# The opening of an attention and MLP mix, reordered: x rounded first, q's second tile moved into the main loop

## The chip, the cores and the metric

The kernel runs on one core of a Trainium2 chip. The core has five engines with an instruction queue each: TensorE (PE, with its weight loads listed apart as PEld), VectorE (DVE), ScalarE (ACT), GpSimd (POOL) and SyncE (SP, which here only issues DMAs). Each queue runs in order, and queues wait for each other through semaphores. The metric is the device time of one execution in microseconds, lower is better. Before the change it is 1294.38 us, the median of three runs.

## The reference

The output mixes two branches of the same input x (2048 positions, 512 features) with a gate per position:

```
g = sigmoid((x * gate_w).sum(-1, keepdims=True))
# branch a: 32 heads of 16 share one k and one v
q = heads(x @ wq);  k = x @ wk;  v = x @ wv
p = softmax(q @ k.T * 16**-0.5)          # 2048 x 2048 for each head
a = (p @ v, heads joined) @ wo
# branch b: 1792 hidden features
r = max(x @ w1 + b1, 0)
b = (r * r) @ w2 + b2
out = g * a + (1 - g) * b
```

All arrays are float32. wq and wk are scaled up by about 36, so scores are large and the softmax needs a shift.

## The kernel before, in words

Products are made in split form: each operand is rounded to the matmul's float format (the r tiles) and the rest of it is kept in a second tile (the l tiles); a product is three matmuls, r by r, l by r and r by l. `xsplit` does this for x (L271): ACT writes xr, and DVE or POOL subtracts to get xl. `wq_split` (L375) does the same for a quarter of wq.

The opening, L386 to L424, is written out in order, and that order is the order on each queue. x comes in four chunks of 512 positions. `kv` (L277) makes k, v and the gate's product for a chunk by 12 matmuls, and three ACT copies of the result: its square, `kvs` and `kb`. `k_parts` (L288) writes the chunk of `k_aug`, the weights of the scores. `kv_rest` (L296) makes the norms of k and turns v over by narrow matmuls, and DVE copies v into `v_ext` and the gate's sums into `z`. The maximum over all norms of k gives the softmax's shift, `km2`, which `k_shift` (L292) writes into rows of k_aug: no score can be made before all four chunks' norms are known.

q is made in tiles of 128 features (8 heads) by one chunk (L312, `qproj`): 12 matmuls, a rounding, a rest, a square, and stores to DRAM (`qs`). `qnorm` (L339) makes q's norms with one matmul and an approximate root and stores them too. `q_load` (L355) reads a group of four heads back in six DMAs, as the scores need it (`qa`). Sixteen tiles of q serve 32 groups. Two tiles, q0 and q1, are made in the opening ("early", with whole matmuls); the other fourteen are made among the scores, with matmuls in pairs on the two halves of the array (`mm2`).

The main loop (L683 to L704) goes over 1024 units, 32 for each group. A unit is `scores` (L496: two matmuls and one exp on ACT) and later its share of `context` (L510). It runs in phases: a phase takes one small chore from a list (`chores`), then two or three units' scores with a piece of the other work between them (`work`, L605: q's tiles, then the MLP, then the output product), then the context of the units of the phase before. A generator says after each piece whether the next phase takes three units (FULL) or two (LIGHT). TensorE runs what it is given in that order. PSUM holds two scores tiles (`sp`), one context accumulator (`ap`) and three others (`mp`).

Before the opening's first real matmul stand 12 matmuls on zeros (`WARM`, L389), which write the accumulator's bank.

Of the kernel before, what the change touches and what calls it, by code (L numbers as in the profile page):

```python
# [135 lines left out]
def mix_kernel(ctx: ExitStack, tc: tile.TileContext, xT, wkv, wq, wo, w12, b1, b2, cst, out):  # L136
# [29 lines left out]
    def pairs(ar, al, br, bl):  # L166
        return [(ar, br), (ar, bl), (al, br)]
# [51 lines left out]
    with fast, tc.tile_pool(name="at", bufs=1) as at, \  # L219
# [7 lines left out]
        xf = {}  # L227

        def x_load(c):
            for a in range(2):  # L230
                if a == 0:
                    both = at.tile([128, KT, CH], F32, name="xf", tag="e", bufs=3)
# [12 lines left out]
        x_load(3)  # L245
        wq_load(slice(128, D))
# [12 lines left out]
        nc.vector.memset(ones, 0.0)  # L259
        nc.vector.memset(ones[:16], 1.0)  # L260
        nc.vector.memset(v_ext, 1.0)

        def run(gen):
            while True:
# [3 lines left out]
                    return e.value  # L268


        def xsplit(c):  # L271
            for a, eng in enumerate((nc.vector, nc.vector if c < 2 else nc.gpsimd)):
                ks = slice(2 * a, 2 * a + 2)
                nc.scalar.activation(xr[c][:, ks], xf[c, a], AF.Copy)
                eng.tensor_tensor(xl[c][:, ks], xf[c, a], xr[c][:, ks].bitcast(F32), OP.subtract)

        def kv(c):  # L277
            ps = mp.tile([128, CH], F32, name="mm")
            mm(ps, [t for k in range(KT) for t in pairs(wkr[:, k], wkl[:, k], xr[c][:, k], xl[c][:, k])])
            kvs = at.tile([128, CH], F32, name="kvs", tag="h", bufs=2)  # L280
            kb = at.tile([128, CH], F32R, name="kb", tag="of", bufs=8)
            sq = at.tile([96, CH], BF, name="sqk", tag="sq", bufs=2)
            nc.scalar.activation(sq, ps[:96], AF.Square)
            nc.scalar.activation(kvs, ps, AF.Copy)
            nc.scalar.activation(kb, kvs, AF.Copy)
            return kvs, kb, sq

        def k_parts(c, kvs, kb, sq):  # L288
            nc.vector.scalar_tensor_tensor(k_aug[:, c * CH:(c + 1) * CH], kb.bitcast(F32), cs[:, C_A:C_A + 1], kvs,
                                           op0=OP.mult, op1=OP.add)  # L290

        def k_shift(c):  # L292
            for p in (RS, 64 + RS):
                nc.vector.tensor_copy(k_aug[p:p + 1, c * CH:(c + 1) * CH], km2[p:p + 1, 0:1].to_broadcast([1, CH]))

        def kv_rest(c, kvs, kb, sq):  # L296
            pn = sp.tile([128, 2, CH], F32, name="s")
            nc.tensor.matmul(pn[:, 0], ones, sq, start=True, stop=True)
            for j in range(4):
                nc.tensor.matmul(pn[:, 1, j * 17:(j + 1) * 17], kvs[:, j * 128:(j + 1) * 128],  # L300
                                 cs[:, C_SEL:C_SEL + 17], start=True, stop=True)
            nc.vector.tensor_reduce(kmx[:, c:c + 1], pn[:, 0], AX.X, OP.max)
            vz = pn[:, 1, :68].rearrange("p (j d) -> p j d", j=4)
            nc.vector.tensor_copy(v_ext[:, 4 * c:4 * c + 4, 0:32:2], vz[:, :, :DH])
            nc.vector.tensor_copy(z[:, 4 * c:4 * c + 4], vz[:, :, DH])

        def root(dst, src, tmp):

            nc.vector.tensor_scalar(tmp.bitcast(I32), src.bitcast(I32), 0.5, ROOT, op0=OP.mult, op1=OP.add)
            nc.vector.tensor_copy(dst, tmp)  # L310

        def qproj(c, t, early=False):  # L312
            cols = slice(t * 128, (t + 1) * 128)
            terms = [u for k in range(KT) for u in
                     pairs(wqr[:, k, cols], wql[:, k, cols], xr[c][:, k], xl[c][:, k])]
            qr = at.tile([128, CH], F32R, name="qr", tag="of", bufs=8)
            ql = at.tile([128, CH], F32R, name="ql", tag="of", bufs=8)
            sq = at.tile([128, CH], BF, name="sq", bufs=2)
            if early:
                q = mp.tile([128, CH], F32, name="mm")  # L320
                mm(q, terms)
                nc.scalar.activation(qr, q, AF.Copy)
            else:
                ps = [mp.tile([128, CH], F32, name="mm") for _ in range(2)]
                yield from mm2(*ps, terms, 6)
                q = at.tile([128, CH], F32, name="qf", tag="of", bufs=8)
                nc.vector.tensor_copy(q, ps[0])
# [3 lines left out]
            nc.vector.tensor_tensor(sq, qr.bitcast(F32), qr.bitcast(F32), OP.mult)  # L331
            it = c * NG + 2 * t
            for src, row, eng in ((qr, 0, nc.sync), (ql, DH + 1, nc.sync if early else nc.gpsimd)):
                o = qs[it, 0, row]
                eng.dma_start(bass.AP(tensor=o.tensor, offset=o.offset,
                                      ap=[[KS * 2 * CH, 4], [CH, 2 * DH], [1, CH]]), src.bitcast(F32))
            return it, sq

        def qnorm(it, sq):  # L339
            p8 = mp.tile([128, CH], F32, name="mm")  # L340
            nc.tensor.matmul(p8[:8], blk, sq, start=True, stop=True)  # L341
            nrm = at.tile([8, CH], F32R, name="nrm", bufs=2)
            tmp = at.tile([8, CH], F32, name="tmp", tag="n")
            nc.vector.tensor_copy(tmp, p8[:8])
# [30 lines left out]
        def wq_split(t, eng):  # L375
            cols = slice(t * 128, (t + 1) * 128)
            nc.scalar.activation(wqr[:, :, cols], wqf[:, :, cols], AF.Copy)
            eng.tensor_tensor(wql[:, :, cols], wqf[:, :, cols], wqr[:, :, cols].bitcast(F32), OP.subtract)

        def gate():  # L380
            for o, s in ((g, -1.0), (omg, 1.0)):
# [3 lines left out]

        wu = at.tile([128, CH], BF, name="wu", tag="sq", bufs=2)  # L386
        nc.vector.memset(wu, 0.0)
        pw = ap.tile([128, CH], F32, name="acc")
        for _ in range(WARM):  # L389
            nc.tensor.matmul(pw, wu[:, :128], wu, start=True, stop=True)  # L390
        split(wkr, wkl, wkvf)
        xsplit(0)
        nc.vector.tensor_copy(blk, cs[:, C_BLK:C_BLK + 8])
        xsplit(1)
        k0 = kv(0)
        k_parts(0, *k0)
        wq_split(0, nc.vector)
        xsplit(2)
        k1 = kv(1)
        kv_rest(0, *k0)  # L400
        xsplit(3)
        k_parts(1, *k1)
        q0 = run(qproj(0, 0, early=True))
        k2 = kv(2)
        kv_rest(1, *k1)
        k3 = kv(3)
        qnorm(*q0)
        kv_rest(2, *k2)
        kv_rest(3, *k3)
        nc.vector.tensor_reduce(km, kmx, AX.X, OP.max)  # L410
        root(km2, km, km2)
        nc.vector.tensor_scalar(km2, km2, -1.0, None, op0=OP.mult)
        for c in range(2):
            k_shift(c)
        for t in range(1, 4):
            wq_split(t, nc.gpsimd)
        q_load(0)
        k_parts(2, *k2)
        k_shift(2)
        q1 = run(qproj(0, 1, early=True))  # L420
        k_parts(3, *k3)
        k_shift(3)
        gate()
        w_load(0)  # L424


        chores = []

        def by_now(what, f):
            while f not in what:  # L430
# [223 lines left out]

        side, lazy = [], work()

        def phase(us):
# [30 lines left out]
        while us:  # L688
# [4 lines left out]
            kind = phase(nxt)  # L693
            if k == 0:
                acc = ap.tile([128, CH], F32, name="acc")
            while narrow:
# [72 lines left out]
```

## Time and profile before

| what | us |
|---|---|
| median of three runs | 1294.38 (1293.84 to 1295.3) |
| the profiled execution, its own time | 1294.1 |
| its span, first to last instruction | 1292.2 |
| TensorE busy | 1263.2 (98%) |
| ScalarE busy | 1030.8 (80%) |
| VectorE busy | 625.8 (48%) |
| GpSimd busy | 58.9 (5%) |
| both halves of the first scores, start | 38.09 |

Times in the profile are counted from the span's start; an instruction's line (L503) is that of the kernel. In the chain of waits each step is what released the next. In groups of instructions the columns are line, engine, operation, output and inputs with shapes, count, busy us and mean ns, and then the engine's idle time ahead of them and what ended it. The timeline gives the start, the length, and the same names, with the idle time in brackets.

### The profile page before, as it was taken

How to read it: one execution, taken by the hardware profiler on the slowest of the kernel's cores; microseconds unless marked ns; L12 is line 12 of the kernel's file. 1: busy time of each engine (PE TensorE's matmuls, PEld its weight loads, DVE VectorE, ACT ScalarE, POOL GpSimd, SP SyncE). 2: the span in 40 equal slices, each digit the busy share in tenths (PEclk: the TensorE clock that was granted, in tenths of full speed). 3: DMA queues.
4: the chain of work that ended last, by engine and by line, in shares of the span. 5: the costliest groups of instructions: out<-in, count | busy, mean ns of one | idle time of the engine just before them, and what ended most of it. 6: DMA issues, size and time to landing. Idle time of an engine off the chain costs nothing.

```text
span 1292.2 us, 25244 instructions
## 1 busy us (share of the span) xinstructions
PE 1263.2 (98%) x10722; PEld 642.5 (50%) x10722; DVE 625.8 (48%) x1117; ACT 1030.8 (80%) x1084; POOL 58.9 (5%) x66
## 2 busy tenths in 40 slices
PE   8899999999999999999999999999999999999996
PEld 5455555555555555555555555555554433322232
DVE  6567855546555464464645547457580304020212
ACT  5677787777877777777777777877779999999984
POOL 2010150200000000000000000000000000000000
PEclk9899999999999999999999999999999999999998
DMA  6233311000101000110011000121001120110100
GB/s 207 79 92 90 93 39 38 30 14 34 38 22 47 15 27 26 39 46 15 16 38 38 30 14 33 38 88 62 18 13 39 46 78 31 53 38 22 54 1 35
DMA packets 29661, 57.36 MB, mean 44 GB/s; under 512 B 8936, under 2 KB 10600, under 8 KB 29544
## 3 DMA queue, kind: packets, MB, share of 16 engines
q1 hardware_dynamic: 23288, 44.40, 10.6%
q0 software_dynamic: 5968, 10.77, 2.6%
q8 instruction: 86, 1.41, 0.4%
q10 hardware_dynamic: 288, 0.52, 0.1%
q14 instruction: 31, 0.25, 0.1%
HBM read 31.02 MB, written 16.78 MB: 37 GB/s over the span
## 4 chain that ended last, share of the span: by engine, by line
PE 91%; ACT 5%; DVE 1%; DMA 1%; issue 1%; SPq 0%; ACTq 0%; DVEq 0%
PE acc L518 35%; PE mm L179 30%; PE s L503 23%; ACT e L507 5%; PE mm L171 1%; DMA xf<-in_xT 1%; DMA qa<-qs 1%; PE mm L341 0%; PE s L171 0%; DMA qs<-nrm 0%; DVE res L468 0%; PE mm L568 0%; PE s L300 0%; ACT accs L545 0%; DVE al L541 0%
## 5 line engine op out<-in xcount | busy, mean ns | idle before, releaser
L507 ACT ACTIVATE e<-s 128x1024 f32<-128x1024 f32 x1024 | 998.5, 1024 | 228.4 <-PE s L503 178.9
L518 PE MATMUL acc<-e,v_ext 128*32 128x512 f32 (+1 forms) x5128 | 524.8, 514 | 0.7 <-ACT e L507 0.7
L503 PE MATMUL s<-qa,k_aug 49*128 49x512 f32 x2048 | 452.5, 439 | 13.0 <-ACT e L507 9.5
L503 PEld LDWEIGHTS s<-qa,k_aug 49*128 49x128 f32 x2048 | 193.7, 184 | 329.7 <-ACT e L507 217.2
L518 PEld LDWEIGHTS acc<-e,v_ext 128*32 128x32 f32 x5128 | 129.2, 108 | 223.4 <-issue 194.3
L468 DVE SCALAR_TENSOR_TENSOR res<-mm,omg,res 128x512 f32<-128x512 f32 x224 | 168.2, 751 | 132.7 <-PE mm L179 119.6
L449 DVE TENSOR_SCALAR h<-mm,b1t 128x512 f32<-128x512 f32 x56 | 42.0, 751 | 208.1 <-PE mm L179 208.1
L179 PE MATMUL mm<-w2r,hr 64*128 64x512 f32 x448 | 91.5, 397 | 0.1
L179 PE MATMUL mm<-w2l,hr 64*128 64x512 f32 x448 | 90.3, 392 | 0.0
L179 PE MATMUL mm<-w2r,hl 64*128 64x512 f32 x448 | 89.7, 390 | 0.0
L179 PE MATMUL mm<-xr,w1l 64*128 64x512 f32 x448 | 88.7, 393 | 0.0
L179 PE MATMUL mm<-xr,w1r 64*128 64x512 f32 x448 | 88.2, 391 | 0.0
L179 PE MATMUL mm<-xl,w1r 64*128 64x512 f32 x448 | 88.2, 390 | 0.0
L209 DVE SCALAR_TENSOR_TENSOR ot<-mm,g,res 128x512 f32<-128x512 f32 x12 | 9.0, 752 | 120.2 <-PE mm L179 120.2
L532 DVE RECIPROCAL n<-n 128x128 f32<-128x128 f32 x60 | 57.2, 953 | 2.1
L529 DVE TENSOR_SCALAR n<-lc 128x128 f32<-128x128 f32 x60 | 13.3, 221 | 75.8 <-DMA lc<-accs 75.3
L179 PEld LDWEIGHTS mm<-w2r,hl 64*128 64x128 f32 x448 | 43.4, 184 | 10.4
L179 PEld LDWEIGHTS mm<-w2l,hr 64*128 64x128 f32 x448 | 43.8, 187 | 8.9
L561 POOL DMA_DIRECT2D oTs<-oc x15 | 8.3, 551 | 871.2 <-DVE oc L533 861.1
L179 PEld LDWEIGHTS mm<-xl,w1r 64*128 64x128 f32 x448 | 42.5, 186 | 9.7
L179 PEld LDWEIGHTS mm<-w2r,hr 64*128 64x128 f32 x448 | 44.2, 187 | 5.9 <-DVE res L468 0.9
L179 PEld LDWEIGHTS mm<-xr,w1l 64*128 64x128 f32 x448 | 41.9, 184 | 9.5
(127 smaller groups left out, 776.6 us busy)
## 6 DMA issues: line engine op xcount, KB each, us to landing
qa<-qs SPq DMA_DIRECT2D x128, 64.0 KB
wf<-in_w SPq DMA_DIRECT2D x14, 512.0 KB
qa<-qs SPq DMA_DIRECT2D x64, 68.0 KB
xf<-in_xT SPq DMA_DIRECT2D x8, 512.0 KB
qs<-qr SPq DMA_DIRECT2D x16, 256.0 KB
oc<-accs SPq DMA_DIRECT2D x30, 128.0 KB
lc<-accs SPq DMA_DIRECT2D x30, 128.0 KB
oTs<-oc POOLq DMA_DIRECT2D x15, 256.0 KB, 2.3
```

Of the source, the lines that this page charges most:

```text
L171: nc.tensor.matmul(ps, a, b, start=first and i == 0, stop=last and i == len(terms) - 1)
L179: nc.tensor.matmul(ps, a[rows], b[rows], start=i == 0, stop=i == len(terms) - 1)
L209: nc.vector.scalar_tensor_tensor(ot, ps[0], g[:, s:s + 1], res[c][:, j], op0=OP.mult, op1=OP.add)
L449: nc.vector.tensor_scalar(h, ps[0], b1t[:, f:f + 1], None, op0=OP.add)
L468: nc.vector.scalar_tensor_tensor(res[c][:, j], p, omg[:, s:s + 1], res[c][:, j], op0=OP.mult, op1=OP.add)
L503: nc.tensor.matmul(s[:, r].rearrange("p (a n) -> p a n", a=2), k_aug[rows, kt * 128:(kt + 1) * 128], qa[it][rows, :, cols], start=True, st ...
L507: nc.scalar.activation(es[u // 2][:, :, cols], s.rearrange("p r (a n) -> p (r a) n", a=2), AF.Exp, scale=SCALE)
L518: nc.tensor.matmul(acc[h * 32:(h + 1) * 32, cols], v_ext[:, i % NK], es[i][:, h % 2 * 2 + h // 2, cols], start=(i % NK == 0), stop=(i % NK ...
L529: nc.vector.tensor_scalar(n[:, cols], l[:, cols], L_MIN, L_MAX, op0=OP.max, op1=OP.min)
L532: nc.vector.reciprocal(n[:, cols], n[:, cols])
L561: nc.gpsimd.dma_start(oTs[it - 1:it + 1].rearrange("u d n -> (u d) n"), o)
```

## The change

The opening is rewritten; the main loop's body is nearly the same.

- x: the fourth chunk gets a buffer of its own (tag "r3"), so that all loads are issued ahead; wq's first quarter is loaded right after x's first chunk. All subtractions for xl and wql are on DVE; three memsets go to POOL.
- Order: k's chunk 0, then q0 at once, then the other chunks; a chunk's matmuls come in two halves, and the roundings of x are put between them. The load of q's first group, `q_load(0)`, is issued before k's third and fourth chunks are done.
- q0's square is made by ACT; the root is taken straight from PSUM, without a copy first.
- v's narrow matmuls write the accumulator's bank (`pv`), and the copies into v_ext and z stand together at the end of the opening.
- The matmuls on zeros are 24 of 240 columns, in the same bank beside `pv` (`pw`), and 24 more stand at the end of the opening, ahead of the first scores.
- Only chunk 0 of k_aug is written in the opening. Chunks 1 to 3, the third and fourth quarter of wq and the gate become chores of the first five phases.
- q1 is no longer made early: `work` begins with it, as the first of fifteen tiles.
- The loop begins with two units instead of three, and the first phase puts its first scores after a piece of q1's matmuls.

```diff
+            both = keep.tile(sh, F32, name="xf", tag="r3") if c == NC - 1 else \
+                at.tile(sh, F32, name="xf", tag="e", bufs=3)
...
         x_load(0)
+        wq_load(slice(0, 128))
         nc.sync.dma_start(cs, cst)
         x_load(1)
-        wq_load(slice(0, 128))
...
+        def kv(c, a):
+            if a == 0:
+                pks[c] = mp.tile([128, CH], F32, name="mm")
+            mm(pks[c], [t for k in (2 * a, 2 * a + 1)
+                        for t in sorted(pairs(wkr[:, k], wkl[:, k], xr[c][:, k], xl[c][:, k]),
+                                        key=lambda t: t[1] is xl[c])], first=a == 0, last=a == 1)
+        def kv_out(c):
+            sq = at.tile([96, CH], BF, name="sqk", tag="sq", bufs=2)
+            nc.scalar.activation(sq, pks[c][:96], AF.Square)
+            kvs[c] = at.tile([128, CH], F32, name="kvs", tag="of", bufs=8)
+            nc.scalar.activation(kvs[c], pks[c], AF.Copy)
+            return sq
...
+        def v_part(c):
+            for j in range(4):
+                nc.tensor.matmul(pv[:, c, j * 17:(j + 1) * 17], kvs[c][:, j * 128:(j + 1) * 128],
+                                 cs[:, C_SEL:C_SEL + 17], start=True, stop=True)
+        def v_out(c):
+            vz = pv[:, c].rearrange("p (j d) -> p j d", j=4)
+            nc.vector.tensor_copy(v_ext[:, 4 * c:4 * c + 4, 0:32:2], vz[:, :, :DH])
+            nc.vector.tensor_copy(z[:, 4 * c:4 * c + 4], vz[:, :, DH])
...
             if early:
                 nc.scalar.activation(qr, q, AF.Copy)
+                nc.scalar.activation(sq, qr.bitcast(F32), AF.Square)
...
-            nc.vector.tensor_copy(tmp, p8[:8])
-            root(nrm, tmp, tmp)
+            root(tmp, p8[:8])
+            nc.vector.tensor_copy(nrm, tmp)
...
+        ps = ap.tile([128, CH], F32, name="acc")
+        pv, pw = ps[:, :272].rearrange("p (c n) -> p c n", c=NC), ps[:, 272:]
+        def warm(n):
+            for _ in range(n):
+                nc.tensor.matmul(pw, wu[:, :128], wu[:, 272:], start=True, stop=True)
+        warm(2 * WARM)
         split(wkr, wkl, wkvf)
+        xsplit(0, 0)
+        xsplit(0, 1)
+        kv(0, 0)
+        kv(0, 1)
+        wq_split(0)
+        xsplit(1, 0)
+        xsplit(1, 1)
+        sq0 = kv_out(0)
         nc.vector.tensor_copy(blk, cs[:, C_BLK:C_BLK + 8])
+        xsplit(2, 0)
         q0 = run(qproj(0, 0, early=True))
+        kv(1, 0)
+        kv(1, 1)
+        k_norm(0, sq0)
+        xsplit(2, 1)
         qnorm(*q0)
+        xsplit(3, 0)
+        sq1 = kv_out(1)
+        kv(2, 0)
+        k_norm(1, sq1)
+        xsplit(3, 1)
+        q_load(0)
+        kv(2, 1)
+        sq2 = kv_out(2)
+        kv(3, 0)
+        k_norm(2, sq2)
+        kv(3, 1)
+        k_parts(0)
+        wq_split(1)
+        sq3 = kv_out(3)
+        for c in range(3):
+            v_part(c)
+        k_norm(3, sq3)
         nc.vector.tensor_reduce(km, kmx, AX.X, OP.max)
...
+        k_shift(0)
+        v_part(3)
+        for c in range(NC):
+            v_out(c)
+        warm(2 * WARM)
+        w_load(0)
+        def k_rest(c):
+            k_parts(c)
+            k_shift(c)
+        chores = [lambda: k_rest(1), lambda: k_rest(2), lambda: (k_rest(3), wq_split(2)), lambda: wq_split(3), gate]
...
-            prev = q1
-            for i in range(2, 16):
+            prev = None
+            for i in range(1, 16):
                 q = yield from qproj(*divmod(i, 4))
-                narrow.append(prev)
+                if prev:
+                    narrow.append(prev)
...
-            if us:
+            if us and not start:
                 scores(us.pop(0))
...
-        kind = FULL
+        kind = LIGHT
```

More of the change, by code (lines that the diff above doesn't have):

```diff
@@ L258, in mix_kernel @@
         z = at.tile([128, NS], F32, name="z")
-        nc.vector.memset(ones, 0.0)
-        nc.vector.memset(ones[:16], 1.0)
-        nc.vector.memset(v_ext, 1.0)
+        nc.gpsimd.memset(ones, 0.0)
+        nc.gpsimd.memset(ones[:16], 1.0)
+        nc.gpsimd.memset(v_ext, 1.0)
         def run(gen):
@@ L268, in run @@
                     return e.value
[L271 to L280, printed above, removed]
-            kb = at.tile([128, CH], F32R, name="kb", tag="of", bufs=8)
[L282 to L286, printed above, removed]
@@ L288, in k_parts, with xsplit @@
-        def k_parts(c, kvs, kb, sq):
-            nc.vector.scalar_tensor_tensor(k_aug[:, c * CH:(c + 1) * CH], kb.bitcast(F32), cs[:, C_A:C_A + 1], kvs,
-                                           op0=OP.mult, op1=OP.add)
+        def xsplit(c, a):
+            ks = slice(2 * a, 2 * a + 2)
+            nc.scalar.activation(xr[c][:, ks], xf[c, a], AF.Copy)
+            nc.vector.tensor_tensor(xl[c][:, ks], xf[c, a], xr[c][:, ks].bitcast(F32), OP.subtract)
+        kvs, pks, pn = {}, {}, []
+        def kv(c, a):
[4 more added lines that the diff above has]
+                                        key=lambda t: t[1] is xl[c])], first=a == 0, last=a == 1)
@@ new lines, in kv_out, with k_parts @@
+        def kv_out(c):
[4 more added lines that the diff above has]
+            return sq
+        def k_parts(c):
+            kb = at.tile([128, CH], F32R, name="kb", tag="of", bufs=8)
+            nc.scalar.activation(kb, kvs[c], AF.Copy)
+            nc.vector.scalar_tensor_tensor(k_aug[:, c * CH:(c + 1) * CH], kb.bitcast(F32), cs[:, C_A:C_A + 1],
+                                           kvs[c], op0=OP.mult, op1=OP.add)
@@ L294, in k_shift, with k_norm, root @@
                 nc.vector.tensor_copy(k_aug[p:p + 1, c * CH:(c + 1) * CH], km2[p:p + 1, 0:1].to_broadcast([1, CH]))
-        def kv_rest(c, kvs, kb, sq):
-            pn = sp.tile([128, 2, CH], F32, name="s")
-            nc.tensor.matmul(pn[:, 0], ones, sq, start=True, stop=True)
+        def k_norm(c, sq):
+            if c < 2:
+                pn.append(sp.tile([128, 2, CH], F32, name="s"))
+            p = pn[c % 2][:, c // 2]
+            nc.tensor.matmul(p, ones, sq, start=True, stop=True)
+            nc.vector.tensor_reduce(kmx[:, c:c + 1], p, AX.X, OP.max)
+        def v_part(c):
             for j in range(4):
-                nc.tensor.matmul(pn[:, 1, j * 17:(j + 1) * 17], kvs[:, j * 128:(j + 1) * 128],
+                nc.tensor.matmul(pv[:, c, j * 17:(j + 1) * 17], kvs[c][:, j * 128:(j + 1) * 128],
                                  cs[:, C_SEL:C_SEL + 17], start=True, stop=True)
-            nc.vector.tensor_reduce(kmx[:, c:c + 1], pn[:, 0], AX.X, OP.max)
-            vz = pn[:, 1, :68].rearrange("p (j d) -> p j d", j=4)
+        def v_out(c):
+            vz = pv[:, c].rearrange("p (j d) -> p j d", j=4)
             nc.vector.tensor_copy(v_ext[:, 4 * c:4 * c + 4, 0:32:2], vz[:, :, :DH])
             nc.vector.tensor_copy(z[:, 4 * c:4 * c + 4], vz[:, :, DH])
-        def root(dst, src, tmp):
-            nc.vector.tensor_scalar(tmp.bitcast(I32), src.bitcast(I32), 0.5, ROOT, op0=OP.mult, op1=OP.add)
-            nc.vector.tensor_copy(dst, tmp)
+        def root(dst, src):
+            nc.vector.tensor_scalar(dst.bitcast(I32), src.bitcast(I32), 0.5, ROOT, op0=OP.mult, op1=OP.add)
         def qproj(c, t, early=False):
@@ L373, in w_split, with wq_split @@
             split(*dst[f], wf[f][:, half * 512:half * 512 + 512])
-        def wq_split(t, eng):
+        def wq_split(t):
             cols = slice(t * 128, (t + 1) * 128)
             nc.scalar.activation(wqr[:, :, cols], wqf[:, :, cols], AF.Copy)
-            eng.tensor_tensor(wql[:, :, cols], wqf[:, :, cols], wqr[:, :, cols].bitcast(F32), OP.subtract)
+            nc.vector.tensor_tensor(wql[:, :, cols], wqf[:, :, cols], wqr[:, :, cols].bitcast(F32), OP.subtract)
         def gate():
@@ L387, in mix_kernel @@
         nc.vector.memset(wu, 0.0)
-        pw = ap.tile([128, CH], F32, name="acc")
-        for _ in range(WARM):
-            nc.tensor.matmul(pw, wu[:, :128], wu, start=True, stop=True)
-        split(wkr, wkl, wkvf)
-        xsplit(0)
-        nc.vector.tensor_copy(blk, cs[:, C_BLK:C_BLK + 8])
[L394 to L402, printed above, removed]
+        ps = ap.tile([128, CH], F32, name="acc")
@@ L410, in mix_kernel @@
+        k_parts(0)
[4 more added lines that the diff above has]
+        k_norm(3, sq3)
         nc.vector.tensor_reduce(km, kmx, AX.X, OP.max)
-        root(km2, km, km2)
+        root(km2, km)
         nc.vector.tensor_scalar(km2, km2, -1.0, None, op0=OP.mult)
-        for c in range(2):
-            k_shift(c)
[L415 to L420, printed above, removed]
@@ L655, in mix_kernel, with phase @@
         side, lazy = [], work()
-        def phase(us):
+        def phase(us, start):
             us = list(us)
@@ L692, in mix_kernel @@
             nxt = units(us[-1] + 1, kind)
-            kind = phase(nxt)
+            kind = phase(nxt, us[0] == 0)
             if k == 0:
```

15 lines of the change are left out of this document (2 added, 13 removed).

## The prediction

> **What bounds the kernel now.** I read the page first (busy shares, the row of slices), then the chain of waits of the first 45 us, then the timeline there by engine, the windows for the granted clock, and the tail's timeline.
>
> ```profile
> span 1292.2 us, 25244 instructions
> PE 1263.2 (98%) x10722; PEld 642.5 (50%) x10722; DVE 625.8 (48%) x1117; ACT 1030.8 (80%) x1084; POOL 58.9 (5%) x66
> ```
>
> The span is TensorE's: 29 us of it are idle, and most of those stand at the two ends. What can be won lies in the first 45 us; what is put behind them is paid on TensorE. The chain there (start, length, what):
>
> ```profile
> 9.92 1.24 DVE xl L275
> 11.20 4.44 PE mm L171 x17
> 15.64 0.23 PE s L298
> 15.87 0.80 PE s L300 x8
> 16.67 5.66 PE mm L171 x24
> ...
> 26.60 0.69 DVE tmp L344
> ...
> 27.76 0.43 DVE nrm L310
> 28.20 2.13 DMA qs<-nrm
> ...
> 31.45 6.50 DMA qa<-qs
> ...
> 38.09 0.78 PE s L503
> ```
>
> The first scores (L503) can run on both halves of the array only at 38.09, when the last load of qa has landed, 7.6 us after q's norms were in DRAM (30.33). q's second tile (12 matmuls) lies inside that wait and costs nothing now. The clock does cost: in the windows the third entry from the end, PEclk, is what TensorE was granted; after each "x" in brackets stands a count, before it the busy time of PE, PEld, DVE, ACT and POOL.
>
> ```profile
> 26.60:30.00 3.40, 2.93 (x20) 2.25 (x19) 3.30 (x11) 3.27 (x6) 1.06 (x1) 1.00 0.26 82
> 30.00:33.40 3.40, 3.13 (x7) 2.48 (x8) 3.23 (x6) 0.00 (x0) 2.86 (x3) 0.50 0.29 83
> 33.40:36.90 3.50, 1.35 (x5) 0.57 (x3) 3.36 (x7) 0.80 (x3) 0.00 (x0) 0.99 0.11 31
> 36.90:40.30 3.40, 1.52 (x5) 0.78 (x5) 2.36 (x8) 1.42 (x2) 0.00 (x0) 0.50 0.66 208
> 40.30:43.60 3.30, 3.18 (x14) 2.14 (x14) 0.00 (x0) 2.58 (x4) 0.00 (x0) 0.50 0.36 119
> 43.60:47.00 3.40, 3.40 (x34) 1.80 (x32) 0.00 (x0) 2.47 (x3) 0.00 (x0) 0.99 0.18 68
> ```
>
> The clock changes in steps of about 3.4 us, and each step follows the one before it: a sparse window (1.35 of 3.50 us; also 2.93 of 3.40 that holds the norms and narrow 17-column matmuls) is followed by half clock, a dense one by full clock. So the first scores of today run at half clock until 43.6.
>
> **The change, part by part.** Rows for the prices, from the groups (mean ns after the bar) and from the timeline (start, length):
>
> ```profile
> L274 ACT ACTIVATE xr<-xf 128x1024 fp32r<-128x1024 f32 x8 | 8.2, 1051 | 6.6 <-DMA xf<-in_xT 6.6
> L275 DVE TENSOR_TENSOR xl<-xf,xr 128x1024 fp32r<-128x1024 f32 x6 | 7.4, 1226 | 5.8 <-ACT xr L274 5.7
> L302 DVE TENSOR_REDUCE kmx<-s 128x1 f32<-128x512 f32 x4 | 2.7, 676 | 0.0
> L285 ACT ACTIVATE kb<-kvs 128x512 fp32r<-128x512 f32 x4 | 2.5, 632 | 0.1
> L283 ACT ACTIVATE sqk<-mm 96x512 bf16<-96x512 f32 x4 | 2.3, 583 | 3.9 <-PE mm L341 2.3 <-PE s L298 1.7
> L377 ACT ACTIVATE wqr<-wqf 128x512 fp32r<-128x512 f32 x4 | 2.3, 615 | 0.0
> L378 DVE TENSOR_TENSOR wql<-wqf,wqr 128x512 fp32r<-128x512 f32 x1 | 0.7, 687 | 0.0
> ```
>
> ```profile
> 2.04 4.76 PE L390 MATMUL acc<-wu 128*128 128x512 bf16 x12 [2.04 <-DVE wu L387]
> 14.56 0.75 DVE L289 SCALAR_TENSOR_TENSOR k_aug<-kb,cs,kvs 128x512 fp32r<-128x512 f32 x1 [0.40 <-ACT kb L285]
> 24.20 0.56 SPq L335 DMA_DIRECT2D qs<-ql  x1
> 29.50 0.20 DVE L304 COPY v_ext<-s 128x64 f32<-128x64 f32 x1
> 29.64 0.14 DVE L305 COPY z<-s 128x4 f32<-128x4 f32 x1
> 37.75 0.85 DVE L294 CAST k_aug<-km 1x512 fp32r<-1x512 f32 x2
> ```
>
> *Loads.* q's first weights (256 KB) go ahead of x's second chunk, which lands some 0.7 us later; x's fourth chunk no longer waits for a buffer. Both are covered: chunk 0 is still first, so k's chunk 0 ends at 12.5 as now, and 24 further matmuls at 5.66/24 = 0.236 keep TensorE busy till 18.1. The memsets on POOL: nothing waits for them before 18. Twice as many warm-ups at 240 of 512 columns take the same 4.8 us at the start.
>
> *Queues and small moves.* SP: q's six qa loads are issued where they were, behind nrm, now with w12's first block and the next qa behind them instead of q1's two stores between; all of these are issued after the first qa, and I take 0 for what they take from it. POOL no longer splits x and wq; its queue holds only q's ql stores. DVE takes over these splits: four of x at 1.23 instead of two, and three more of wq at 0.69; they are in the chains below. The sort inside a chunk's matmuls compares slices with a whole tile and changes no order. The norms' two PSUM tiles are shared by chunks 0 and 2, 1 and 3: a norm waits for the maximum two before it, long done.
>
> *q's norms.* q's tile ends on TensorE at 15.3, k's chunk 1 at 18.1, its norm at 18.4. The new square of q on ACT takes a buffer that the norm's matmul reads, so ACT, with the other roundings queued behind, stands from 16.4 to 18.4; sq ends at 19.0. DVE then has xl (20.05 to 21.3), the root straight from PSUM (0.69) and the cast (0.43): nrm leaves at 22.45, not 28.20. With nrm's 2.13 and the same 7.6, qa would be in at 32.2. But the qa loads need qr and ql in DRAM too, and these leave at 16.4 and 17.8, behind input that keeps the DMA busy to about 20:
>
> ```profile
> 20.00:21.00 1.00, 1.00 (x5) 0.78 (x5) 1.00 (x2) 0.94 (x2) 0.46 (x1) 1.00 0.17 7
> ```
>
> Today ql left at 24.20 and all was in at 30.33, some 6 for one tensor that follows another. Two in a row from 20, at about 4 each, end at 28.2, and qa is in at 35.9. So qa lands between 32.2 and 35.9 against 38.09, and I take the late end, since no row shows the two stores faster.
>
> *k and the second warm-ups.* ACT goes on with xr twice (21.1), two evictions (22.2), xr (23.2). DVE: xl to 23.7, a maximum to 24.4, xl to 25.6. So k's last six matmuls end at 27.0, three v parts at 0.80 at 29.4, the last norm at 29.7, its maximum at 30.4, three tiny operations and the two casts of 0.85 at 31.9, and eight copies of v and z (two rows above: about 0.3 per chunk, against a gap) at 33.2. The program's order then shows what the diff hides: the first of the second 24 warm-ups waits for DVE, for the last of these copies, because they read the PSUM tile that the warm-ups write; the first scores are queued behind the warm-ups. From 27.0 to 33.2 TensorE has only narrow matmuls and a 3.0 us pause: by the windows above it is at half clock. 240 columns take 4.76/12 x 240/512 = 0.19 to 0.20 us each, half that after the clock is back, 2 to 5.4 us into the batch: 3.4 to 4.8 us, 4.2 in the middle. The scores start at **37.4** (36.6 to 38.0; 35.8 at full clock throughout), so the earlier qa is nearly all lost to them. Gain 0.7.
>
> *The first phases.* Steady phases, the tail and DVE's five steps on a q tile:
>
> ```profile
> 48.03 0.69 DVE L327 COPY qf<-mm 128x512 f32<-128x512 f32 x1 [8.62 <-PE mm L179]
> ...
> 49.76 0.50 PE L503 MATMUL s<-qa,k_aug 49*128 49x512 f32 x2
> ...
> 50.63 0.69 DVE L331 TENSOR_TENSOR sq<-qr 128x512 bf16<-128x512 f32 x1
> ...
> 52.07 1.50 PE L518 MATMUL acc<-e,v_ext 128*32 128x512 f32 x16
> 53.49 0.50 PE L503 MATMUL s<-qa,k_aug 49*128 49x512 f32 x2
> ...
> 57.40 0.50 PE L503 MATMUL s<-qa,k_aug 49*128 49x512 f32 x2
> ...
> 1149.57 3.77 ACT L507 ACTIVATE e<-s 128x1024 f32<-128x1024 f32 x4 [0.25 <-PE s L503]
> 1153.59 3.77 ACT L507 ACTIVATE e<-s 128x1024 f32<-128x1024 f32 x4 [0.24 <-PE s L503]
> ```
>
> Two phases (six units, one q tile) take 57.40 - 49.76 = 7.64; contexts of three units 53.49 - 52.07 = 1.42; six q terms 1.4; an exp 0.96 in a row. I count from the start T of the scores, units numbered from 0. Phase 1 (q1's first half, scores 2 and 3, contexts 0 and 1) ends at T+3.8; kb of chunk 1 stands between exp 1 and exp 2. Phase 2 has scores 4 to 6, q1's end and kb of chunk 2 after exp 3: T+7.8. Phase 3 begins q's third tile, whose weights are split in that same phase. On ACT, wqr stands behind exp 6 (T+8.45) and kb of chunk 3 (0.6): T+9.5. On DVE, wql stands behind chunk 2's k_aug (0.75) and casts (0.85), from T+5.65; q1's five steps, 3.2; chunk 3's k_aug and casts; 0.7 of its own: T+12.8. TensorE has its score at T+8.05, waits 1.5 for wqr, does two terms, waits 2.85 for wql, all else queued behind. Phase 3 ends at T+15.7, phase 4 at T+19.5, with 13 units scored, 10 in context, two tiles of q made in phases. The pauses also make a sparse window whatever its offset, hence one at half clock: 1.0 to 2.5 us, I take 1.7. So 37.4 + 19.5 + 1.7 = 58.6.
>
> Today the like state (the same tiles of q, 9 scored, 6 in context) stands at 49.76: 8.8 us earlier with four units fewer. In the tail four units take 1153.59 - 1149.57 = 4.02, which come off there. gate() and later splits lie beside TensorE, 0.
>
> **Sum:** 8.8 - 4.0 = +4.8 on the profiled execution's 1294.1: **1298.9**. (The median of the runs is 1294.4; they spread from 1293.8 to 1295.3, so that some 0.2%, 2.6 us, is what can be told from no change.)
>
> **A rule against this.** The Trainium skill, "TensorE: Matmul & The Clock Gate", section "Why this matters for your kernels", asks only that there be no pauses over about 3 us; by its section "What's actually happening" an idle window of about 3.4 us halves the clock. The window of 26.6 above, with no such pause, disagrees. By that rule the sum would be 1295.6, the first rival's.
>
> **The rivals.**
> 1. *Only a long pause halves the clock.* Then neither the pauses of 1.5 and 2.85 nor that of 3.0 do it: 1.7 less in the phases, 1.6 less in the warm-ups (which then end at 35.8, just ahead of the late qa), 1298.9 - 3.3 = 1295.6, no change. Against it: half clock from 30.0 after a window with 2.93 us busy. Chance 0.13.
> 2. *Not slower: the weights' split is no stall,* if wql comes by T+8.5. Scores then wait for ACT alone (exps, three kb, wqr): phase 4 ends at T+16.0, with no sparse window: 37.4 + 16.0 - 49.76 - 4.02 = -0.4, 1293.7. It decides where DVE has wql within 1 us of wqr. Against it stand 7.1 us of queued DVE work; for it, that DVE is idle 8.62 us ahead of L327 today. Chance 0.12.
> 3. *The scores start as qa lands,* at 33.2 rather than 37.4, if the chain to the last copy is some 4 us shorter (sq's wait for the norm and the evictions behind it are 2 us each of it): 1298.9 - 4.2 = 1294.7. Against it, each of these waits stands in the order of the queues. Chance 0.10.
> 4. *Faster:* 2 with 3, 1293.7 - 4.2 = 1289.5. Chance 0.13.
>
> **How the numbers follow.** The forecast has the remaining 0.52; its own range is 1296.5 to 1301.5 (start 36.6 to 38.0, clock 1.0 to 2.5, a stall 1 us shorter or longer). Slower by over 2.6 us is the forecast and 0.05 from the upper ends of rivals 1 and 3: 0.57. Faster is rival 4 and 0.02 from the lower end of 2: 0.15. The rest is no change: 0.28. The range from 1291.5 to 1301.5 holds rivals 1 to 3 and leaves out rival 4 below and a later start above.
>
> **What would show it.** nrm leaves near 22.5 and qa lands between 32 and 36; the second warm-ups begin right after the last z copy, near 33, at about 0.2 us each; the scores follow at 36.6 to 38. In the first phases TensorE stands some 4 us in all for wqr and wql, and PEclk falls to 0.5 near 50. Wrong it would be if the warm-ups end before qa lands, if the wait for wql is under 1 us, or if the tail does not give back 1 us a unit.

## The result, and the profile after

The changed kernel takes 1305.94 us (median of six runs, 1305.71 to 1306.99) against 1294.12 for the kernel before in the same comparison: a ratio of 1.0092, 95% interval 1.0079 to 1.0105. That is 11.8 us slower where 4.8 were forecast, and outside the range. The profiled execution took 1305.84.

The first lines of the page after:

```profile
span 1304.0 us, 25104 instructions
...
PE 1269.4 (97%) x10658; PEld 643.3 (49%) x10658; DVE 619.4 (48%) x1104; ACT 1031.0 (79%) x1084; POOL 51.4 (4%) x65
```

TensorE has 64 matmuls fewer in all (more warm-ups, but fewer pieces of contexts, since the sets of units fall otherwise), is 6.2 us longer busy and 5.6 longer idle. "Busy" does not mean that nothing was lost there: one group below grew by 5.6 us of busy time with the same number of matmuls at nearly the same mean duration.

The opening in the timeline after (start, length, what; the idle time ahead of it in brackets), first SyncE, then TensorE:

```profile
22.66 0.65 SPq L362 DMA_DIRECT2D qs<-nrm  x1
24.73 4.08 SPq L375 DMA_DIRECT2D qa<-qs  x6
```

```profile
32.93 3.94 PE L408 MATMUL acc<-wu 128*128 128x240 bf16 x24 [2.35 <-DVE z L319]
36.80 0.73 PE L537 MATMUL s<-qa,k_aug 49*128 49x512 f32 x4
...
46.01 0.50 PE L179 MATMUL mm<-xr,wqr 64*128 64x512 f32 x2 [0.93 <-ACT wqr L392]
...
49.48 0.79 PE L179 MATMUL mm<-xr,wql 64*128 64x512 f32 x2 [2.74 <-DVE wql L393]
...
57.84 0.50 PE L537 MATMUL s<-qa,k_aug 49*128 49x512 f32 x2
```

and the window behind the two waits (the third entry from the end is the granted clock):

```profile
49.30:52.70 3.40, 3.22 (x16) 2.03 (x20) 0.13 (x1) 1.27 (x2) 0.00 (x0) 0.50 0.30 99
```

This is what the prediction drew. The scores start at 36.8, TensorE stands for wqr and then wql, the clock falls to a half, and the state reached at 49.76 before is reached at 57.84. From there the forecast took the loop as unchanged. It is not. The same work, found in both timelines: the first and last squaring of h in the MLP (the maximum with 0, times h), the last eviction of the output product's chunk 2, and the first of the last four. After:

```profile
162.63 0.69 DVE L485 SCALAR_TENSOR_TENSOR h<-h 128x512 f32<-128x512 f32 x1
...
952.30 0.69 DVE L485 SCALAR_TENSOR_TENSOR h<-h 128x512 f32<-128x512 f32 x1
...
1148.93 0.75 DVE L209 SCALAR_TENSOR_TENSOR ot<-mm,g,res 128x512 f32<-128x512 f32 x1 [11.11 <-PE mm L179]
...
1294.16 0.75 DVE L767 SCALAR_TENSOR_TENSOR ot<-s,g,most 128x512 f32<-128x512 f32 x1 [1.43 <-PE s L171]
```

and before:

```profile
155.70 0.69 DVE L451 SCALAR_TENSOR_TENSOR h<-h 128x512 f32<-128x512 f32 x1
...
938.85 0.69 DVE L451 SCALAR_TENSOR_TENSOR h<-h 128x512 f32<-128x512 f32 x1
...
1133.44 0.75 DVE L209 SCALAR_TENSOR_TENSOR ot<-mm,g,res 128x512 f32<-128x512 f32 x1 [11.11 <-PE mm L179]
...
1282.45 0.75 DVE L732 SCALAR_TENSOR_TENSOR ot<-s,g,most 128x512 f32<-128x512 f32 x1 [1.43 <-PE s L171]
```

The lag is 6.93 us where the MLP begins, 13.45 where it ends, 15.49 behind the output product, and 11.71 at the end, when the four units scored ahead come off. So 6.5 us are lost inside the MLP and 2.0 behind it.

Where in the MLP, the groups tell (busy us and mean ns, then TensorE's idle time ahead of them). After (with a row of the output product), and before:

```profile
L179 PE MATMUL mm<-w2r,hr 64*128 64x512 f32 x448 | 97.1, 399 | 2.7 <-DVE res L502 2.7
...
L179 PE MATMUL mm<-wor,orr 64*128 64x512 f32 x120 | 23.8, 393 | 1.0 <-DVE orr L163 1.0
```

```profile
L179 PE MATMUL mm<-w2r,hr 64*128 64x512 f32 x448 | 91.5, 397 | 0.1
```

The group has grown that opens each step of the second product. (The two terms behind it, w2l,hr and w2r,hl, grew by 4.5 and 3.6 us as well, because one half of the array now runs behind the other there; the groups overlap in time, so these figures do not add up.) From the starts of all matmuls between the first and the last squaring of h, summed by pairs of neighbours, the interval between two neighbours that are both w2r,hr (the two halves of the array) takes 8.50 us after and 2.43 before: 6.07 of the 6.5. These matmuls write PSUM banks that DVE must have evicted. One place of ten, on DVE and on TensorE, after:

```profile
241.52 0.75 DVE L483 TENSOR_SCALAR h<-mm,b1t 128x512 f32<-128x512 f32 x1 [2.18 <-PE mm L179]
242.38 0.69 DVE L484 TENSOR_TENSOR h<-h,mm 128x512 f32<-128x512 f32 x1
...
244.29 0.69 DVE L164 TENSOR_TENSOR hl<-h,hr 128x512 fp32r<-128x512 f32 x1
244.90 0.22 DVE L563 TENSOR_SCALAR n<-lc 128x128 f32<-128x128 f32 x1
...
245.49 0.95 DVE L566 RECIPROCAL n<-n 128x128 f32<-128x128 f32 x1
246.47 0.29 DVE L567 TENSOR_TENSOR oc<-oc,n 128x128 f32<-128x128 f32 x1
246.68 1.61 DVE L502 SCALAR_TENSOR_TENSOR res<-mm,omg,res 128x512 f32<-128x512 f32 x2
```

```profile
246.89 0.40 PE L179 MATMUL mm<-w2r,hr 64*128 64x512 f32 x1
247.48 0.50 PE L179 MATMUL mm<-w2r,hr 64*128 64x512 f32 x1 [0.20 <-DVE res L502]
```

and the same place before, on DVE:

```profile
237.02 0.69 DVE L164 TENSOR_TENSOR hl<-h,hr 128x512 fp32r<-128x512 f32 x1
238.06 1.62 DVE L468 SCALAR_TENSOR_TENSOR res<-mm,omg,res 128x512 f32<-128x512 f32 x2 [0.34 <-PE mm L179]
239.59 0.22 DVE L529 TENSOR_SCALAR n<-lc 128x128 f32<-128x128 f32 x1
```

Before, DVE finishes a hidden tile, evicts the first step of the second product, and then divides a quarter of a finished attention tile (`pieces` and `divide`, L529 to L533). After, the divide, some 1.8 us from 244.90, stands ahead of that eviction. The evictions start at 246.68, and the next step's matmul, due at 246.9 and a pair with its neighbour, waits till 247.48. The dearest two of the ten places are at 571 and 808 us, with intervals of 1.66 and 1.42 us: there a split of w1 stands on DVE between the divide and the eviction.

Nobody moved the divide. `pieces` begins a fixed three phases after a group's end and then takes every second phase. The MLP's pattern is eight phases long: two hidden tiles of two phases each and four steps of the second product of one each. The change puts q's tile 1 into the work, which is two phases more, and begins the scores with sets of two, so that the first group has 12 sets and not 11. So a group now ends one phase earlier against the MLP's pattern. The divide has gone from the even to the odd phases, and stays there, since eight is even.

### The profile page after: what moved, and what is told of

Read it like the earlier page. It is cut to its first block, busy times and chain, and to the rows that moved or that the text cites. A ratio compares the mean times of both kernels' runs of the same rounds, so it can differ in the third digit from the quotient of the medians.

```text
span 1304.0 us, 25104 instructions
## 1 busy us (share of the span) xinstructions
PE 1269.4 (97%) x10658; PEld 643.3 (49%) x10658; DVE 619.4 (48%) x1104; ACT 1031.0 (79%) x1084; POOL 51.4 (4%) x65
## 4 chain that ended last, share of the span: by engine, by line
PE 90%; ACT 5%; DVE 3%; DMA 1%; issue 1%; SPq 0%; ACTq 0%; DVEq 0%
PE acc L552 34%; PE mm L179 30%; PE s L537 23%; ACT e L541 4%; PE mm L171 1%; DMA oT<-oTs 1%; DMA xf<-in_xT 0%; PE mm L356 0%; PE acc L408 0%; DVE n L566 0%; ACT xr L274 0%; PE s L171 0%; DVE res L502 0%; PE acc L313 0%; DVE h L483 0%
## 5 line engine op out<-in xcount | busy, mean ns | idle before, releaser
L552 PEld LDWEIGHTS acc<-e,v_ext 128*32 128x32 f32 x5016 | 125.3, 108 | 221.0 <-issue 195.3
L179 PE MATMUL mm<-w2r,hr 64*128 64x512 f32 x448 | 97.1, 399 | 2.7 <-DVE res L502 2.7
L179 PE MATMUL mm<-w2l,hr 64*128 64x512 f32 x448 | 94.8, 394 | 0.0
L179 PE MATMUL mm<-w2r,hl 64*128 64x512 f32 x448 | 93.3, 390 | 0.0
L179 PEld LDWEIGHTS mm<-w2r,hr 64*128 64x128 f32 x448 | 46.9, 186 | 11.8 <-DVE res L502 6.8
L179 PEld LDWEIGHTS mm<-w2r,hl 64*128 64x128 f32 x448 | 46.3, 184 | 10.3
L179 PEld LDWEIGHTS mm<-xr,w1r 64*128 64x128 f32 x448 | 42.4, 186 | 5.1
```

What stands on the lines that cost most here:

```text
L179: nc.tensor.matmul(ps, a[rows], b[rows], start=i == 0, stop=i == len(terms) - 1)
L552: nc.tensor.matmul(acc[h * 32:(h + 1) * 32, cols], v_ext[:, i % NK], es[i][:, h % 2 * 2 + h // 2, cols], start=(i % NK == 0), stop=(i % NK ...
```

## The experiments

All edits are to the changed kernel unless said otherwise; a ratio is to the kernel before, in the same comparison.

**The divide one phase later, and two.**

```diff
-            for _ in range(3):
+            for _ in range(4):
                 yield
```

> The changed kernel with one edit: the division of a finished pair of groups begins four phases after its second group, not three. In the changed kernel q's tile 1 takes two more phases of the work and the first group has one set more, so each group ends one phase earlier against the MLP's steps than before; the divide's 1.76 us on DVE now stand between the five steps of a hidden tile (3.2 us) and the first evictions of the second product, whose PSUM banks TensorE then waits for. Theory P (the phase decides): one phase later gives the order of before back; the 6.0 us lost between consecutive matmuls of the second product go, and the 1.0 us wait for orr and part of the rest behind it too: 1298 to 1300.2 us, and TensorE's wait for the evictions of L502 falls under 1 us. Rival W (the loss follows from more work standing behind four more scored units, wherever the divide is): 1305.9, within 1 us. Rival D (DVE stands at the divide's head for the DMA that brings lc): a gain too, but then the next run, two phases later, gains as much.

> The changed kernel with the division five phases after its group, two later than it has. Theory P: a hidden tile and a step of the second product take two phases each, so the divide stands in the same kind of phase as with three, and the loss stays: 1304.5 to 1306.5. Rival D (the wait for lc's DMA at the divide's head): that wait is gone here as with four phases, and both gain 6 to 8 us: 1298 to 1300. Rival W: 1305.9 within 1 us, like P; the run before tells these two apart.

One phase later: 1299.75 us, 1.0040 (1.0027 to 1.0054), 6.2 less than the changed kernel. Two phases later (`range(5)`): 1308.2 us, 1.0103 (1.0088 to 1.0119), 2.3 more. The rows of the second product, with one phase and with two:

```profile
L179 PE MATMUL mm<-w2r,hr 64*128 64x512 f32 x448 | 91.7, 397 | 0.5 <-DVE res L502 0.5
```

```profile
L179 PE MATMUL mm<-w2r,hr 64*128 64x512 f32 x448 | 96.1, 398 | 4.5 <-DVE res L502 4.5
```

The loss goes and comes back as the phase's parity says. That excludes a loss from the work's being late as such (it would not move), and DVE's wait for the DMA of lc at the divide's head (it would stay away with two). The second is 1.7 above its range. By the starts of the squarings, it is already 1.8 us behind the changed kernel where the MLP begins, its scores having started 1.7 later. The MLP costs it 1.75 us more, nearly all of that at one place (336 us) that the changed kernel passes, where a split of w1 stands behind the divide. Behind the MLP 1.15 us come back. (A step of the second product takes one phase, not two as that expectation has it; its conclusion hangs only on the pattern's even length.) The wait for orr in the output product, 1.0 us, stayed (1.2), and so did 1.5 of the 2.0 us lost behind the MLP: most of these are not the divide's. The eighth kernel, below, takes them away too.

**The kernel before, with the divide one phase later** (the same edit there).

> The kernel before with the division four phases after its group instead of three, nothing else changed: its opening is the old one. Theory P: the divide moves into the phases that it has in the changed kernel, and the old kernel loses what the changed one lost in its loop: 6 to 8 us, 1300 to 1302. Rivals W and D: no loss, 1294.1 within 1 us, or a little faster.

1301.96 us, 1.0057 (1.0044 to 1.0071). The old kernel, with the old opening, loses 7.5 us by this one number:

```profile
L179 PE MATMUL mm<-w2r,hr 64*128 64x512 f32 x448 | 96.5, 399 | 3.9 <-DVE res L468 3.9
```

**wq's third quarter split earlier.**

```diff
-        chores = [lambda: k_rest(1), lambda: k_rest(2), lambda: (k_rest(3), wq_split(2)), lambda: wq_split(3), gate]
+        chores = [lambda: k_rest(1), lambda: wq_split(2), lambda: k_rest(2), lambda: wq_split(3), lambda: k_rest(3), gate]
```

> The changed kernel with the pieces of the first phases in another order: the split of wq's third quarter stands alone in the second phase, ahead of the rests of k's chunks 2 and 3, which go to the third and fifth phase. The prediction's step of the first phases: TensorE's waits for wqr (0.93 us) and wql (2.74 us) go, and with them the sparse window behind them and the 3.4 us at half clock (1.7 us): 3.7 + 1.7 less up to 1 us for exps that are then the limit of those phases, 1300.5 to 1302. Rival: the exps and the half-clock start keep phases 1 to 4 as long, and 2 us or less come of it, 1304 to 1305.9. The loss in the loop is not touched: the wait for L502's evictions stays.

1301.62 us (1299.18 to 1302.45), 1.0048 (1.0034 to 1.0062): 4.3 less. In the profiled run the scores start at 39.66, x's first chunk having come late (its second half was rounded at 9.38, in the changed kernel at 7.74), and the third tile of q goes through without a wait or a slow clock:

```profile
39.66 0.73 PE L537 MATMUL s<-qa,k_aug 49*128 49x512 f32 x4
...
47.76 0.40 PE L179 MATMUL mm<-xr,wqr 64*128 64x512 f32 x2
48.00 0.40 PE L179 MATMUL mm<-xl,wqr 64*128 64x512 f32 x2
48.23 0.39 PE L179 MATMUL mm<-xr,wql 64*128 64x512 f32 x2
```

From the first score to the first term in wql it is 8.57 us here and 12.68 in the changed kernel. By the starts of the MLP's squarings the run is 2.8 ahead of the changed kernel although its scores began 2.86 later, so the stall and the half clock were worth 5.6, as the steps had it (0.93 + 2.74 + 1.7 = 5.4).

**Both edits together.**

> The changed kernel with both edits: the division four phases after its group and the split of wq's third quarter in the second phase. If the two losses are independent, as the places say (the loop from 250 us on, the first 55 us), they add: 6.2 and 4.3 off 1305.9, 1295.4 (1294.5 to 1296.5), still no better than before by what is lost in the opening itself. If either hides the other, 1298 or more.

1293.63 us, 0.9997 (0.9988 to 1.0006): level with the kernel before, and 0.9 under the expected range. It is 12.3 under the changed kernel, more than the 10.5 of the two medians. The fourth kernel's five runs lie in two clusters, 1299.2 to 1299.7 and 1301.6 to 1302.5; with the lower one the sum is 12.5 to 12.9. With that, the losses add as far as these runs can tell, and with both away nothing is left of the 11.8 us.

**The second warm-ups left out, or in a PSUM tile of their own.** On the kernel with both edits, the one dropping `warm(2 * WARM)`, the other:

```diff
             v_out(c)
+        pw = mp.tile([128, CH], F32, name="mm")[:, 272:]
         warm(2 * WARM)
```

> The run before with the second 24 warm-ups left out (they feed nothing). Prediction's theory, that the first scores stand behind the warm-ups and these behind DVE's last copy of z while qa has long landed: scores at 32 (the end of the casts of km, 31.97) instead of 36.8, the first phases at half clock for one window (1.7 us more), net 2.5 to 3.5 us off the run before: 1292 to 1293. Rival (the prediction's late end for qa, 35.9): the scores wait for qa, gain under 1 us and lose 1.7 to the clock: 1295 to 1297.

> As the run with both edits, the second 24 warm-ups kept, but writing a PSUM tile of their own, so that they follow v's matmuls at 30.6 without waiting for the copies that end at 32.9. They take 2.4 us at full clock to 4.7 at half: scores at 33 to 35.3 and then at full clock; 1.5 to 3.8 us off the run with both edits, 1291.6 to 1294. If qa lands only at 35.9, 0.9 us off at most: 1294.5.

1293.96 (1.0002, 0.9993 to 1.0011) and 1294.30 (0.9998, 0.9989 to 1.0007): both level with the run before, and neither brings what was expected of it (2.5 to 3.5 us and 1.5 to 3.8). Without the warm-ups, TensorE in the timeline, and the windows that follow:

```profile
34.08 0.76 PE L536 MATMUL s<-qa,k_aug 49*128 49x512 f32 x1 [2.27 <-DMA qa<-qs]
37.49 1.19 PE L536 MATMUL s<-qa,k_aug 49*128 49x512 f32 x3 [2.65 <-DMA qa<-qs]
```

```profile
33.80:37.20 3.40, 0.76 (x1) 0.29 (x1) 0.34 (x4) 0.00 (x0) 0.00 (x0) 0.50 0.17 58
37.20:40.60 3.40, 3.11 (x14) 2.81 (x16) 0.00 (x0) 2.31 (x3) 0.00 (x0) 0.50 0.07 27
40.60:44.00 3.40, 3.40 (x17) 1.08 (x14) 1.89 (x4) 2.60 (x4) 0.00 (x0) 0.50 0.07 27
```

So the warm-ups were not what held the scores: without them the first half has its scores at 34.08, but the second not before 37.49, where the run with both edits has both at 37.15. qa lands in two halves, at 34.1 and 37.5 here, although its norms were issued at 23.88, 4.3 us earlier than before the change (28.20). Between the two landings the DMA engines' share (next to last entry) is 0.17, and from 36 to 37 us, just ahead of the second landing, it is 0.06, at 25 GB/s.

**The divide put right by another route.** With wq's split earlier and the divide left at three phases:

```diff
-        kind = LIGHT
+        kind = FULL
         us = units(0, kind)
```

> The changed kernel with wq's split earlier (as in the fourth run) and the scores begun with a set of three units, not two, the division left at three phases. The first group then has 11 sets, as before the change; with q's tile 1 among the phases it ends two phases of the MLP's steps earlier than before the change, an even number, so the divide stands where it stood before by another route than a later start. Theory P: the loop's 6 to 8 us go here too, 1292.5 to 1296. If it was the later start of the divide itself that helped: 1301.6, as the fourth run, within 1 us.

1293.23 us, 0.9993 (0.9984 to 1.0002); and the second product's row is back at its 0.1 us of idle time. The phase decides, not a later start of the divide.

The 2.0 us behind the MLP are gone here as well. From the last squaring of h to the last eviction of chunk 2 it takes 194.4 us, as in the kernel before (194.6; 196.6 in the changed kernel), and TensorE's wait for orr is 0.0. With the groups ending elsewhere in the pattern, this loss is gone too; by what path it arises was not traced.

**What holds qa.** Two kernels with wq's split earlier, the warm-ups in a tile of their own, 12 of them, and w12's first block loaded in the first phase. The first has the divide at four phases; the second has the first set of three and the divide at three.

> As the run with both edits and the warm-ups in a tile of their own, with 12 second warm-ups instead of 24, and w12's first block (512 KB, moved at 188 to 320 GB/s from 30 to 32.5 us while the scores' qa was on its way) loaded in the first phase, behind qa. Theory Q, that this block stands ahead of qa's last parts (in the run without second warm-ups they landed at 34.1 and 37.5): qa is in by 33 to 34.5, the scores start there, 1.5 to 3 us earlier than 36.2, 1290.5 to 1292.8. Rival: qa waits for its own small packets and the next qa, lands after 36 all the same, and the shorter warm-ups cost clock: 1293.5 to 1296.

> The first set of three (division at three phases) with the warm-ups and the block of w12 as in the run before this one. If both theories hold, their gains add to the run with both edits: 1290 to 1293, a version under both kernels; if P alone holds, 1293 to 1296.

1294.11 (1.0001, 0.9992 to 1.0010) and 1293.29 (0.9995, 0.9986 to 1.0004): neither gains what theory Q asks for, and it falls. In the second of them, with the block of w12 behind qa:

```profile
32.72 0.46 PE L537 MATMUL s<-qa,k_aug 49*128 49x512 f32 x1 [2.05 <-DMA qa<-qs]
35.97 1.19 PE L537 MATMUL s<-qa,k_aug 49*128 49x512 f32 x3 [2.79 <-DMA qa<-qs]
```

(In the first of them the second wait, till 36.33, is put down to w12's block, which the scores don't read; which of the two it was is not shown there.) Again there are two landings, 3.25 us apart, and behind the first of them, from 32 to 33 us, the DMA engines are all but idle (0.06). From 34 on w12's block moves beside the second half (0.63 and 0.89). The transfers of qa by kind, and a window of the first of the two kernels:

```profile
qa<-qs SPq DMA_DIRECT2D x2, 64.0 KB
qa<-qs SPq DMA_DIRECT2D x1, 68.0 KB
```

```profile
32.00:33.00 1.00, 0.18 (x1) 0.18 (x1) 0.00 (x0) 0.00 (x0) 0.00 (x0) 1.00 0.06 25
```

A share of 0.06 is one engine of sixteen, at 25 GB/s. A half of qa is two blocks of 16 rows (64 KB each) and one of 17 rows (q's norms and the sixteen of ql, 68 KB); 68 KB at 25 GB/s are 2.8 us, close to the 3.25 to 3.41 between the landings.

**The block of 17 rows as one row and sixteen,** in the first of those two kernels, and in the kernel before.

```diff
-Q_ROWS = (0, 0, DH), (DH, 0, DH), (RS, DH, KS)
+Q_ROWS = (0, 0, DH), (DH, 0, DH), (RS, DH, DH + 1), (RS + 1, DH + 1, KS)
```

> As the run with w12's block behind qa, with one edit: of each half of qa the block of 17 rows (q's norms and ql) is loaded as one row and sixteen. In that run the two halves landed at 32.8 and 36.0 with the DMA engines at a share of 0.06 and 25 GB/s from 31 on, which is one engine of sixteen at work. Theory E: the transfer of 17 rows goes through one engine, each of the two some 3 us; split, qa is in by 32.5, the scores start at the casts' end (31.3) to 32.5 instead of 36.3, with the clock kept up: 4 to 6 us off 1294.1, 1288 to 1290.5. Rival: the time is the latency of the loads' own chain or of another transfer, and the two further issues a load only delay: 1294 to 1296.

> The kernel before with only this edit. Theory E: its first scores, at 38.09 behind the last load of qa (6.5 us after its issue), start 3 to 5 us earlier, less what DVE's casts (38.6 for the second chunk) and q's tile 1 then hold: 1290.5 to 1293. Rival: 1294.4 to 1296.

The first takes **1287.33 us, 0.9949 (0.9935 to 0.9963)**, faster than both kernels; the kernel before with this line alone takes 1289.62, 0.9963 (0.9949 to 0.9977). Both are somewhat below their expected ranges, by 0.7 and 0.9 us. The first scores, in the one and in the other:

```profile
30.03 1.39 PE L408 MATMUL mm<-wu 128*128 128x240 bf16 x12
31.35 0.79 PE L537 MATMUL s<-qa,k_aug 49*128 49x512 f32 x3
```

```profile
34.59 0.47 PE L503 MATMUL s<-qa,k_aug 49*128 49x512 f32 x1
35.97 0.70 PE L503 MATMUL s<-qa,k_aug 49*128 49x512 f32 x3 [0.91 <-DMA qa<-qs]
```

Both halves have scores at 31.35 instead of 36.3, right behind the warm-ups and at full clock, and at 35.97 instead of 38.09. While qa is loaded in the first kernel, more engines are at work:

```profile
28.00:30.00 2.00, 2.00 (x20) 1.97 (x20) 0.58 (x1) 0.00 (x0) 0.00 (x0) 1.00 0.55 129
```

With qa cut, both halves have scores 4.6 us earlier with the new opening than with the old one. Only 2.3 us of that are left between the two medians, and the two intervals overlap: that the early q norms, which the change paid for, now pay is likely but not shown.

## Why the prediction was wrong

- **q's norms** held in the time. nrm leaves at 22.66 (forecast 22.45).
- **When qa lands** was taken at the late end, 35.9, which the runs bear out (second half at 35.97 and 37.49 in two kernels where the wait is put down to qa). The reason given, two stores in a row behind the input, was not it: the transfers of 17 rows were.
- **The second warm-ups** held in the times, not in the blame. They begin at 32.93 (33.2), take 3.94 (4.2), the scores start at 36.80 (37.4). That "the earlier qa is nearly all lost to them" is wrong: without them the second half of qa still has no scores before 37.49.
- **The first phases** held. TensorE waits 0.93 for wqr (1.5) and 2.74 for wql (2.85), and wql comes 12.68 after the first score (12.8). 57.84 stands for 58.6, 8.1 us late for 8.8. With the split moved, 5.6 came back.
- **The tail** held: 15.49 - 11.71 = 3.78 given back for 4.02.
- **The step that failed is the term for the loop, put at nothing.** Behind the first phases the prediction has only "gate() and later splits lie beside TensorE, 0", and carries the lag found there unchanged to the tail. By its own terms as measured, 8.1 - 3.8 = 4.3 us would have come out, on the forecast of 4.8. The other 7.5 are the loop's: 6.5 in the MLP, of which 6.07 are waits for evictions behind a divide that changed places (shown by the first, second, third and eighth kernels), and 2.0 in the output product (1.0 a wait for orr, the rest not traced; the eighth kernel has neither), less 1.1 us by which the lag shrank among q's tiles, from 8.1 to 6.9. The prediction counted the four units and the extra tile as amounts of work, and did not ask what they do to the order in which the loop's fixed delays fall.
- **Rival 1 and the rule behind it** fall. The longest pause in front of the half clock of 49.3 was 2.74 us. The Trainium skill, "TensorE: Matmul & The Clock Gate", section "Why this matters for your kernels", asks only for no gaps over some 3 us; the measurement decides against it here.
- **The prediction's own rule for the clock,** that a sparse window is followed by half clock and a dense one by full clock, gave the right term here but is too simple. In the changed kernel the window from 42.50 to 45.92 has 2.38 us of busy time of 3.42, and the next is at full clock. Nor do the rows say how busy a window must be to bring the full clock back: without second warm-ups the one from 37.2 did not (3.11 us of 3.40), in the changed kernel the one from 49.3 did (3.22).
- **Rivals 2 to 4** needed a wql or scores some 4 us earlier, and neither was.

## What to carry to other kernels

Where a helper generator runs a fixed number of phases behind an event, a change in how many steps stand ahead of that event can move it against everything else on its engine for the rest of the kernel; compare the order of the instructions on that engine in the steady loop, before and after, and not only where the edit is. A wait that a change removes is worth something only if the next one does not stand at the same time: take the next one away too, alone and together, before blaming either. When a transfer is late while the DMA engines' share is one sixteenth, look at its shape, not at what else is moving.

## What the runs showed of the hardware

A load of 17 rows of 4 KB goes through one DMA engine: a share of 0.06 and 25 GB/s while nothing else moves. Cut into one row and sixteen, qa came early enough to gain 6.8 us in one kernel (medians, 1294.11 to 1287.33) and 4.3 in the other (1293.93 to 1289.62). The Trainium skill, "DMA: Bandwidth & Descriptors", section "Why a DMA increments its semaphore by 16 and not by 1", says that the number of engines is the largest up to 16 that divides the slowest dimension (of those that are not 1) on both sides. For 17 that is 1 and for 16 it is 16, and the trace agrees: a share of 0.06 with the 17 rows, and of 0.55 at 129 GB/s with the cut loads. The loads of qa for the other 31 groups had the same shape, but they are issued a group ahead, and the MLP did not feel it: from its first squaring to its last the kernel before takes 783.2 us with either shape, and the other kernel 784.3 and 784.4. Behind the MLP the kernel before did not feel it either (194.6 us). In the other kernel 1.3 us of the gain lie there (195.9 to 194.6), where the wait for orr, 1.1 us, is 0.0 with the cut loads; that the loads' shape did this is not shown.
